# Column-tiled broadcasts of the second modulation, a new dense order, and a moved last norm in a fused attention and token-mixing kernel

## The chip, the cores and the metric

The kernel runs on one core of one Trainium2 chip. The metric is the device time of one execution in microseconds, lower is better. Before the change three runs took 251.43, 252.77 and 253.32 us; the median is 252.77. One profiled execution took 251.73 us, of which the profile's span (first to last instruction) is 250.0; times inside the profile are counted from the start of the span.

## The reference

One transformer-like block over x of 2048 rows by 512 columns (bf16), with six modulation vectors from a conditioning vector c:

```python
mod = (silu(c) @ w_mod).reshape(1, 6, 1, 512)
sa, ca, ga, sb, cb, gb = mod[:, 0], ..., mod[:, 5]
h = layernorm(x) * (1 + ca) + sa
x = x + ga * A(h)        # A: 32 heads of 16, causal, window of 256 rows, softmax, then @ wo
h = layernorm(x) * (1 + cb) + sb
x = x + gb * B(h)        # B: layernorm again, then u = gelu(w1.T @ h + b1), y = w2.T @ u + b2
```

B mixes rows: w1 is 2048 x 1792 and w2 1792 x 2048, and the 512 columns pass through side by side. So every row block of h (16 blocks of 128 rows) must be there before u is complete, but the sum over the row blocks can be begun with those that are.

## The kernel before

**Stages.** Rows go in 16 blocks of 128 (`tb`), four blocks make a row group (`tg`, 0 to 3). The preamble (to about 13 us) makes the first modulation and the first query and key block. Then comes the attention part (to about 160 us): 76 units, (group, block of 8 heads, piece of the window), in a fixed order. Each unit is: scores on TensorE (`emit_scores`, lines 616 and 628, the latter for the mask), two exponentials of 128x1024 on ScalarE (`emit_exp`, line 639), and after the units of eight heads the values (`emit_av`, line 656), which VectorE transposes and divides by the row sums (`norm_out` line 667, `norm_rest` lines 680 to 691). After 160 us comes the tail: the last four output projections (`t_wo`, lines 1115 and 1119), the last norms (`t1`, `t2`, `t3`), the first product of B (lines 1094 and 1187), GELU (1104), and the second product (line 1211) with the output (1218 to 1224).

**Dense groups.** Between the scores, TensorE is given dense groups, each four matmuls of 128x512 into one of two PSUM banks, and an evacuation: `k`, `q` and `v` blocks (`qk_group`, `v_group`; k12 is group 1, block of heads 2; v7 is row block 7), output projections `wo` of a row block (`wo_group`, line 412; the residual is added at 418), the transposed biases (`bias`), and the broadcasts `bc` (`bc_group`, lines 385 to 397). `ORDER` (line 739) lists them; `run_dense` takes the first of the list that is ready. When none is ready it makes a part sum (`part_group`, line 453): matmuls of w1 by the row blocks of h that are there, for 10 of the 14 column blocks of w1 (`PART`) and row blocks below 10 (`NB`), at least four at a time. What was summed in this way is left out of the sums in the tail. After a `wo` group a chain of small norm steps (`ln23`, lines 696 to 727) makes the row block of h: the norm of the residual, times 1 + cb, plus sb, and the second norm. Its statistics are on VectorE, three small steps on GpSimd (POOL; lines 217, 220, 224), the rest on either.

**The broadcasts.** ga, cb, sb and gb are needed as rows that are the same in all 128 partitions. A group makes each: the conditioning vector, replicated to 128 columns (`sT_rep`, line 583), is the stationary operand, and a 512-wide part of w_mod moves, so all 128 output rows are equal. VectorE copies the result (adding 1 for cb). ga is then folded into the projection weights (`fold_wod`, line 947, four operations), cb and sb are used in `ln23`, gb at line 1218. A `wo` group needs the folded weights, cb and sb.

**The planner.** The order of instructions is written at build time by a planner (`Plan`) with a clock for each engine (`pl.pe`, `pl.dve`, `pl.pool`, `pl.sp`) and prices for each step; `ready` holds when a result is expected. `fill` runs chain steps on VectorE until a given time, `drain` the evacuations, `force` makes what the next unit needs. All loads and copies by DMA are issued by SP in program order; an instruction on SP that waits holds up those behind it. The keys of head blocks 2 and 3 of groups 1 to 3 are copied into the `KT` ring by eight DMAs (line 369), the value blocks are swapped between partition halves by two (line 313), the normed rows are transposed by DMA (line 301), and w1 is loaded where other weights have been used up (lines 965 to 983). `PLAN` (line 756) holds six of its settings.

**The end of the attention.** After the last values, the planner ran all leftover chain steps (`while pl.chains: fill(...)`), and then came the tail.

## Time and profile before

| | before |
|---|---|
| three runs, us | 251.43, 252.77, 253.32 |
| profiled execution, us | 251.73 |
| its span, us | 250.0 |
| granted TensorE clock | 0.998 |
| first exponential begins, last ends, us | 13.05, 159.24 |
| exponentials on ScalarE, busy us (line 639) | 139.7 in 152 |
| second product of B on TensorE, chain share (line 1211) | 19% |
| part sums ahead, from ... to, us (line 453) | 121.5 to 158.8 |

Engines are written PE (TensorE), PEld (its weight loads), DVE (VectorE), ACT (ScalarE), POOL (GpSimd), SPq (SyncE, issuing DMAs). In a timeline a row has the start in us, the length in us, engine, line and operation, what it writes and reads, shapes, the number of instructions that were merged, and in brackets how long the engine had been idle and what ended that. A matmul record of 128x512 lasts about 0.38 us, but such matmuls overlap and follow each other every 0.22 us; some records are missing, and weight loads are counted in full.

### The profile page before, as it was taken

What the parts mean: (1) busy time and instruction counts of PE and PEld (TensorE: products, weight loads), DVE (VectorE), ACT (ScalarE), POOL (GpSimd) and SP (SyncE); (2) the same over time, 40 slices, a digit from 0 to 9 for tenths busy, and PEclk for the clock granted to TensorE, in tenths of its full rate; (3) what the DMA queues carried; (4) which work ended last, traced back from release to release, by engine and by line L of the source; (5) the groups of instructions that cost most, each with busy time, mean ns of one, the idle gap of its engine ahead of it and who ended that gap; (6) DMA issues with size and microseconds to landing.
All of it is one profiled execution on the core that took longest, in us unless ns stands there. A gap on an engine that the chain in (4) does not pass through costs nothing.

```text
span 250.0 us, 8264 instructions
## 1 busy us (share of the span) xinstructions
PE 229.4 (92%) x3547; PEld 119.2 (48%) x3585; DVE 181.1 (72%) x363; ACT 160.2 (64%) x183; POOL 108.3 (43%) x222
## 2 busy tenths in 40 slices
PE   6888897999899999899999999979999999999994
PEld 2543554445445545545545545534444444444443
DVE  5988999988799799989899999869624404150643
ACT  2285999998899999999999999703564400000000
POOL 7325462216748629866878789337600000000000
PEclk9999999999999999999999999999999999999999
DMA  5986994064630255000359300699950000111121
GB/s 177 318 265 161 142 326 153 9 127 83 193 139 5 51 91 88 5 3 3 60 84 335 94 0 5 207 393 414 409 200 0 0 0 21 65 41 43 45 84 43
DMA packets 31977, 30.49 MB, mean 122 GB/s; under 512 B 15940, under 2 KB 26564, under 8 KB 31940
## 3 DMA queue, kind: packets, MB, share of 16 engines
q1 hardware_dynamic: 31940, 29.96, 41.2%
q8 instruction: 28, 0.46, 0.7%
q14 instruction: 9, 0.07, 0.1%
HBM read 22.03 MB, written 2.10 MB: 96 GB/s over the span
## 4 chain that ended last, share of the span: by engine, by line
PE 52%; ACT 23%; DVE 11%; SPq 5%; DMA 4%; issue 2%; POOL 2%; POOLq 0%; DVEq 0%; ACTq 0%
ACT et L639 23%; PE py L1211 19%; PE pu L1094 6%; PE pss L616 5%; PE pu L1187 5%; PE dn L453 4%; PE dn L322 4%; PE dn L345 4%; DMA x<-in_A_x_dram 2%; SPq L369 2%; DVE KT L375 2%; DVE t L667 2%; PE pss L628 2%; DVE ln_stats L236 1%; SPq L123 1%
## 5 line engine op out<-in xcount | busy, mean ns | idle before, releaser
L639 ACT ACTIVATE et<-pss 128x1024 bf16<-128x1024 f32 (+1 forms) x152 | 139.7, 1037 | 6.7 <-PE pss L628 6.2
L1211 PE MATMUL py<-guT,w2r 128*128 128x512 bf16 (+1 forms) x234 | 48.3, 366 | 0.2
L616 PE MATMUL pss<-QT,KT 32*128 32x64 bf16 (+3 forms) x720 | 37.2, 254 | 4.7 <-ACT et L639 1.8
L1211 PEld LDWEIGHTS <-w2r 128*128 128x128 bf16 x238 | 23.3, 98 | 25.3
L1218 DVE SCALAR_TENSOR_TENSOR o<-py,bFM,bc_gb 128x512 bf16<-128x512 f32 (+1 forms) x17 | 11.7, 716 | 30.5 <-PE py L1211 30.5
L345 PE MATMUL dn<-h1T,wqkv 128*128 128x512 bf16 x111 | 31.1, 381 | 1.8 <-issue 1.1
L616 PEld LDWEIGHTS <-KT 32*128 32x128 bf16 x720 | 14.2, 92 | 34.3 <-issue 22.7
L217 POOL TENSOR_SCALAR ln_ve<-ln_mv 128x1 f32<-128x1 f32 (+1 forms) x40 | 9.3, 232 | 43.0 <-DVE ln_mv L237 19.9
L667 DVE STREAM_TRANSPOSE t<-pss 128x512 f32<-128x512 f32 x32 | 20.9, 691 | 4.3 <-PE pss L656 4.3
L656 PE MATMUL pss<-et,VaugT 64*32 64x320 bf16 (+4 forms) x720 | 20.8, 253 | 1.1 <-ACT et L639 0.6
L656 PE MATMUL pss<-et,Vx 64*32 64x320 bf16 (+4 forms) x720 | 20.9, 254 | 0.0
L628 PE MATMUL pss<-mask_rown,mask_hown 32*128 32x128 bf16 (+1 forms) x304 | 20.6, 206 | 0.0
L656 PEld LDWEIGHTS <-VaugT 64*32 64x32 bf16 x720 | 18.7, 91 | 3.8 <-issue 3.3
L683 POOL TENSOR_TENSOR merge<-t,zr 128x512 bf16<-128x512 f32 x13 | 13.8, 1059 | 15.4 <-DVE zr L680 15.3
L628 PE MATMUL pss<-mask_rfar,mask_hfar 32*128 32x64 bf16 (+1 forms) x304 | 19.8, 200 | 0.0
L220 POOL TENSOR_TENSOR ln_rb<-ln_ve,mhalf 128x1 f32<-128x1 f32 x32 | 18.3, 572 | 2.7
L656 PEld LDWEIGHTS <-Vx 64*32 64x32 bf16 x720 | 17.8, 91 | 1.4 <-issue 0.6
L322 PE MATMUL dn<-wqkv,h1T 128*128 128x512 bf16 x58 | 16.0, 380 | 2.0 <-DVE sT_rep L583 0.7
L1102 DVE TENSOR_TENSOR gelu_a<-pu,part 128x512 f32<-128x512 f32 x10 | 6.4, 686 | 13.4 <-PE pu L1187 8.2
L453 PE MATMUL dn<-hb,w1hi 128*128 128x512 bf16 x51 | 14.5, 381 | 0.5 <-issue 0.3
L345 PEld LDWEIGHTS <-wqkv 128*128 128x128 bf16 x120 | 9.6, 97 | 10.7 <-DVE KT L375 0.7
L691 DVE STREAM_TRANSPOSE OTd<-merge 128x512 bf16<-128x512 bf16 x16 | 11.2, 699 | 1.2 <-POOL merge L683 1.2
(130 smaller groups left out, 366.9 us busy)
## 6 DMA issues: line engine op xcount, KB each, us to landing
w2r<-in_B_w_dram SPq DMA_DIRECT2D x14, 512.0 KB, 10.2
wmod<-in_w_mod_dram SPq DMA_DIRECT2D x12, 256.0 KB, 4.7
w1b<-in_B_w_dram SPq DMA_DIRECT2D x6, 448.0 KB, 7.3
Vx<-VaugT SPq DMA_DIRECT2D x16, 147.5 KB, 2.5
x<-in_A_x_dram SPq DMA_DIRECT2D x16, 128.0 KB, 3.6
w1hi<-in_B_w_dram SPq DMA_DIRECT2D x6, 320.0 KB, 4.8
out_dram<-otile SPq DMA_DIRECT2D x15, 128.0 KB, 1.7
wqkv<-in_B_w_dram SPq DMA_DIRECT2D x4, 320.0 KB, 3.9
```

What stands on the lines that cost most here:

```text
L220: nc.gpsimd.tensor_tensor(out=r, in0=ve[:], in1=mhalf[:, 0:n], op=ALU.pow)
L322: nc.tensor.matmul(pv[:], lhsT=h1T[tg][:, dc, tl * P : (tl + 1) * P], rhs=wqkv[:, dc, 2 * D : 3 * D], start=(dc == 0), stop=(dc == ND - 1),)
L345: nc.tensor.matmul(pq[:], lhsT=wqkv[:, dc, col0 : col0 + P], rhs=h1T[tg][:, dc, :], start=(dc == 0), stop=(dc == ND - 1),)
L453: nc.tensor.matmul(ps[:], lhsT=w1_of(s0 + n, fc), rhs=hb[s0 + n][:], start=(n == 0), stop=(s0 + n + 1 == s1),)
L616: nc.tensor.matmul(pss[j // 2][:, j % 2, 64 * at : 64 * (at + c1 - c0)], lhsT=Kring[kh // 8 % 3][rows, g8, kh % 8].rearrange("p n t -> p ( ...
L628: nc.tensor.matmul(o[:, at[0] : at[-1] + 1 : step, :], lhsT=mask_h[name][rows].rearrange("p n t -> p (n t)"), rhs=mask_r[name][rows, :].un ...
L639: nc.scalar.activation(out=state["e", tg, g8, ui][:, 2 * a : 2 * a + 2, 0:n], in_=state.pop((u, a))[:, :, 0:n], func=ACT.Exp, scale=SCORE_ ...
L656: nc.tensor.matmul(state["po"][32 * j : 32 * j + 32, par, 64 * c0 : 64 * c1], lhsT=v[:, h * DV : h * DV + 32], rhs=state["e", tg, g8, ui][ ...
L667: nc.vector.transpose(out=state["t2"][:, par, :], in_=state["po"][:, par, :])
L683: eng.tensor_tensor(out=m[:].rearrange("p (b a d) -> p a b d", a=2, d=DH), in0=t2v[:, :, :, 0:DH], in1=zr[:].to_broadcast([P, 2, 16, DH]), ...
L1094: nc.tensor.matmul(pu[fc][:], lhsT=w1_of(sc, fc), rhs=hb[sc][:], start=(sc == done.get(fc, 0)), stop=(sc == NT - 1),)
L1211: nc.tensor.matmul(pys[n][:, c0:c1], lhsT=w2r[:, fc, tb * P : (tb + 1) * P], rhs=guT[fc][:, c0:c1], start=(fc == gelus[0]), stop=(fc == ge ...
```

## The change

1. **Broadcasts.** One group replaces four. Each of its four steps runs four matmuls, one for each of ga, cb, sb and gb, into 32 output columns each at column positions 0, 32, 64 and 96 of the array; `sT_rep` has 32 columns. VectorE copies the bank once, adding 1 in the rows of cb by a per-partition scalar. SP then writes four rows to DRAM and reads them back, replicated to all partitions, into one tile `bc_all`. All four quarters of w_mod and both loads of wo must be there before the group starts.
2. **The order.** A new `ORDER`, new `PLAN` settings, and changed prices of the planner's clocks.
3. **q01 on ScalarE.** The groups named in `PLAN[6]` (here q of group 0, head block 1) are evacuated by an activation with Copy on ScalarE.
4. **The end of the attention.** Of each leftover chain all but its last step run before the tail; the last step (the second norm of a row block, `n3`) runs after the second residual of the tail. Loads that are still listed are issued at the end of the attention.

```diff
-    bc_cb1 = const.tile([P, D], DT.bfloat16, name="bc_cb1")
-    bc_sb = const.tile([P, D], DT.bfloat16, name="bc_sb")
-    bc_gb = const.tile([P, D], DT.bfloat16, name="bc_gb")
+    bc_all = const.tile([P, 4, D], DT.bfloat16, name="bc_all")
+    bc_ga, bc_cb1, bc_sb, bc_gb = (bc_all[:, n, :] for n in range(4))
+    outside = ctx.enter_context(tc.tile_pool(name="outside", bufs=1, space=bass.MemoryType.DRAM))
+    bc_rows = outside.tile([4, D], DT.bfloat16, name="bc_rows")
...
-    sT_rep = modw.tile([P, ND, P], DT.bfloat16, name="sT_rep")
+    sT_rep = modw.tile([P, ND, 32], DT.bfloat16, name="sT_rep")
+    bc_row = modw.tile([P, D], DT.bfloat16, name="bc_row")
+    add_row = modw.tile([P, 1], DT.float32, name="add_row")
+    nc.gpsimd.memset(add_row[:], 0.0)
+    nc.gpsimd.memset(add_row[32:64, :], 1.0)
...
+    def copy_of(key):
+        return functools.partial(nc.scalar.activation, func=ACT.Copy) if key in PLAN[6] else nc.vector.tensor_copy
...
-                nc.vector.tensor_copy(out=QT[tg][g8][:], in_=pq[:])
+                copy_of((kind, tg, g8))(out=QT[tg][g8][:], in_=pq[:])
...
-    def bc_group(v, dst, add1, then=()):
+    BC = (2, 4, 3, 5)
+    def bc_group(then):
         def mm(ps_b, k):
-            nc.tensor.matmul(
-                ps_b[:], lhsT=sT_rep[:, k, :], rhs=wmod_of(v)[:, k, :],
-                start=(k == 0), stop=(k == ND - 1),
-            )
+            for n, v in enumerate(BC):
+                nc.tensor.matmul(
+                    ps_b[32 * n : 32 * n + 32, :], lhsT=sT_rep[:, k, :], rhs=wmod_of(v)[:, k, :],
+                    start=(k == 0), stop=(k == ND - 1), tile_position=(0, 32 * n), skip_group_check=True,
+                )
         def evac(ps_b):
-            if add1:
-                nc.vector.tensor_scalar_add(out=dst[:], in0=ps_b[:], scalar1=1.0)
-            else:
-                nc.vector.tensor_copy(out=dst[:], in_=ps_b[:])
-        return Group(ND, mm, evac, 0.65, [("w", v)] + [("w", "o")] * (v == 2), ("bc", v), then=then)
+            nc.vector.tensor_scalar_add(out=bc_row[:], in0=ps_b[:], scalar1=add_row[:])
+            dma.dma_start(out=bc_rows[:], in_=bc_row[0:P:32, :])
+            dma.dma_start(out=bc_all[:], in_=bc_rows[:].unsqueeze(0).to_broadcast([P, 4, D]))
+        return Group(ND, mm, evac, 0.65, [("w", v) for v in BC] + [("w", "o")], ("bc",), us=0.27, then=then)
...
-            v1 k20 wo3 q31 v2 q10 q22 k21 q33 wo11 wo6 v0 q02 wo0 q21 k11 q30 k10 bc2 v3 k01 v7
-            v6 v15 wo8 q01 q20 bias k33 q32 v10 k13 wo7 wo9 q03 v4 v8 q11 v5 k02 wo5 k12 v9 k31
-            v14 q23 bc3 v13 wo2 k30 bc0 q13 v12 wo10 k22 v11 bc1 wo1 q12 wo4 k32 k23 k03
+            k10 v13 v12 q32 wo4 wo5 bias k20 wo8 q23 q30 wo11 v1 v0 q20 v9 v3 v2 k22 k01 q10 q01
+            k33 k30 v7 k02 v11 q02 v6 v14 v5 k11 v15 q11 wo10 k23 k03 v10 wo9 k13 v4 v8 wo6 wo1
+            q31 q22 q21 k31 q03 k12 q13 k21 bc wo2 wo7 wo3 q12 k32 q33 wo0
...
-        PLAN = (0.2, 8.0, 5.0, 0.4, 0.6, 0.2)
+        PLAN = (2.0, 16.0, 8.0, 0.4, 0.3, 0.2, (('q', 0, 1),))
...
-        ready["w", "b"], pl.sp = 8.0, 5.0
+        ready["w", "b"], pl.sp, pl.dve = 8.0, 5.6, 2.5
...
+                    if g.gives == ("bc",):
+                        issue(pl.dve, 0.65)
+                        pl.sp += 2.0
+                        landed = issue(pl.dve, 0.65) + 0.5
+                        for v in BC:
+                            ready["bc", v] = landed
+                        add_chain(g.then, ready["bc", 2])
+                        return
...
-            pl.pe += 1.1 if tg == 0 else 1.38
+            pl.pe += 1.05 if tg == 0 else 1.33
...
-                st = lambda g: [(lambda tl=tl: ln1_stats(g, tl), 0.82, 0.1, None) + (1.5,) * (tl % 2) for tl in range(4)]
+                st = lambda g: [(lambda tl=tl: ln1_stats(g, tl), 0.85, 0.1, None) + (1.5,) * (tl % 2) for tl in range(4)]
...
-                pl.pe += 0.37
-                scored = pl.pe + 0.25
+                pl.pe += 0.33 if late else 0.4
+                scored = pl.pe + 0.22
...
         emit_av(NG - 1, ND - 1, (4,), False, True)
+        while loads:
+            o, i, key = loads.pop(0)
+            dma.dma_start(out=o, in_=i)
         norm_out(0)
...
-        while pl.chains:
-            fill(pl.dve + 9.0)
+        while any(len(chain[0]) > 1 for chain in pl.chains):
+            for chain in pl.chains:
+                if len(chain[0]) > 1:
+                    run(chain)
...
         for step in range(5):
             if step < 4:
                 t_wo(12 + step)
+            if step == 1:
+                for chain in pl.chains:
+                    run(chain)
             if step:
                 t1(11 + step)
```

Not shown: the prices of the dense evacuations (0.65 to 0.66, masked keys 1.35 to 1.33, the fold 0.33 to 0.40), the clock of ScalarE's copy in the planner, and the places that read the broadcasts, which now read parts of `bc_all`.

## The prediction

> **What bounds the kernel now.** I read the page's busy table first, then ScalarE's timeline, then a table of stretches, then the two groups of matmuls that matter, the chain of waits, and last the timelines around 23 and 166 us.
>
> ```profile
> span 250.0 us, 8264 instructions
> ...
> PE 229.4 (92%) x3547; PEld 119.2 (48%) x3585; DVE 181.1 (72%) x363; ACT 160.2 (64%) x183; POOL 108.3 (43%) x222
> ```
>
> TensorE is busy 92% of the span, 20.6 us idle. In the attention part (13 to 160 us) ScalarE looks like the bound: its exponentials, by its timeline:
>
> ```profile
> 23.93 21.03 ACT L639 ACTIVATE et<-pss 128x1024 bf16<-128x1024 f32 x24 [2.97 <-PE pss L628]
> 45.18 14.86 ACT L639 ACTIVATE et<-pss 128x1024 bf16<-128x1024 f32 x16 [0.21 <-PE pss L628]
> 61.08 3.77 ACT L639 ACTIVATE et<-pss 128x1024 bf16<-128x1024 f32 x4 [1.04 <-PE pss L628]
> 65.86 93.38 ACT L639 ACTIVATE et<-pss 128x1024 bf16<-128x1024 f32 x100 [1.01 <-PE pss L628]
> ```
>
> The brackets are the idle time before each piece: with 0.45 and 0.24 at the start, 5.9 us in all. But a gap of ScalarE isn't by itself a gap of the kernel. While ScalarE waits, TensorE works on dense groups, and what it does not get done before 160 us it does after. The stretches show how full it is in the end of the attention:
>
> ```profile
> 125.00:140.00 15.00, 14.68 (x289) 7.64 (x295) 13.94 (x28) 14.96 (x17) 11.63 (x21) 1.00 0.73 203
> 140.00:150.00 10.00, 9.71 (x229) 5.33 (x224) 9.10 (x18) 9.96 (x12) 8.18 (x15) 1.00 0.06 16
> 150.00:160.00 10.00, 9.74 (x263) 5.61 (x264) 9.60 (x20) 9.19 (x10) 7.86 (x14) 1.00 0.19 56
> ```
>
> (Columns: length, busy PE, PE weight loads, DVE, ACT, POOL, granted clock, DMA.) TensorE is at 97 to 98%, VectorE at 91 to 96%, at full clock. The filler there is line 453, part sums of the MLP's first product, made ahead:
>
> ```profile
> L453 PEld LDWEIGHTS <-w1hi x56: 95/98/99, 121.5 to 157.9; 128*128 128x128 bf16 x56
> ...
> L453 PEld LDWEIGHTS <-wqkv x19: 95/98/99, 145.9 to 158.6; 128*128 128x128 bf16 x19
> ```
>
> 75 weight loads, so 75 such matmuls, of the 100 that the code allows (10 column blocks times 10 row blocks): 25 more could be made ahead. After 160 us the chain is TensorE's own to the end. So the time is TensorE's work plus its idle time, and a slot saved in the attention shortens the tail by one slot. The price of a slot is in the chain, 10.74 / 49 = 0.219 us, with the price of packed small matmuls ahead of it:
>
> ```profile
> 159.16 1.36 PE pss L656 x95
> ...
> 173.39 10.74 PE pu L1094 x49
> ```
>
> **Part 1, the broadcasts on TensorE.** Removed: four groups of four matmuls of 128x512 (line 387: 16 weight loads, 14 records), 16 x 0.219 = 3.50 us. Added: four steps of four matmuls, each 32 output columns wide, side by side. The trace has no four-column tiles over 128 rows; the nearest row is line 656, eight tiles of 64 rows by 32 columns. One such group has 12 pieces with 2560 columns in all for each of eight tiles; one after another they would take 8 x 2560 x 0.219 / 512 = 8.76 us, and the chain shows 1.36: 6.4 of 8, or 80%. So a step costs 0.219 / 0.8 = 0.274, four cost 1.10, saved 2.40. Bounds: full overlap saves 3.50 - 0.88 = 2.6; no overlap saves nothing, and if each of 16 loads (98 ns, this line's row) then stands free too, it loses 1.6. I take 2.4, because line 656 has the same column tiles.
>
> In the Trainium skill, "TensorE: Matmul & The Clock Gate", Part 3, says that weight loads overlap running matmuls only where their row groups differ. By that rule these four tiles, which share all rows, would gain less, down to nothing. The trace speaks against it: at 159.25 to 159.40 loads of line 656 for column tiles of the same row half run while matmuls that began at 159.24 last until 159.54. The rule as a rival is below.
>
> The 2.40 us become 2.40 / 0.219 = 11 more part sums ahead; the room is 25. Cover: VectorE must empty them (0.69 us for each group of 4 or more). It gains its own time: evacuations 0.692 + 0.692 + 0.679 + 0.675 = 2.74 become one of 0.68; the copy that replicates the conditioning vector (0.42) shrinks to a quarter of its elements (nearest 128x128 rows 0.34, so 0.1 saved); the copy of q01 (0.68) leaves. That is 2.8 us, four evacuations' worth, so the 11 sums are covered, and I book nothing more for VectorE. Without this cover the 2.4 is 0.
>
> **Part 2, the broadcasts by DMA.** SP issues one write to DRAM and one replicating read. Issues on SP cost 0.4 to 0.6 each; a write to DRAM lands in 1.5 to 1.7 us (the output's rows); the second waits on SP for the first, and 0.5 MB to 128 partitions takes 3.7 (0.25 MB of wod) to 7.3 (0.45 MB of w1b), I take 5. So SP stands 0.6 + 1.7 + 0.6 = 2.9 us, and the fold of wod begins about 8 us after the evacuation. Before, all four broadcasts were out at 59.6 and the first of line 412's projections ran at 62.5. All four quarters of wmod were issued by 35.9, so the group can run from about 41. If it does, SP's queue is empty (nothing issued from 37.2 to 48.6) and the wait costs nothing. If it runs between 48 and 64, four transposes, four swaps and the eight copies into KT (56.71 to 63.82) stand behind it. Nothing, then, to 2.9; I take 0. The fold itself keeps its four operations (median 0.42).
>
> **Part 3, the norm behind the residuals.** VectorE and TensorE at the seam:
>
> ```profile
> 164.75 0.18 DVE L706 BATCH_NORM_AGGREGATE ln_mv<-ln_stats 128x2 f32<-128x6 f32 x1
> 166.28 0.41 DVE L228 TENSOR_SCALAR hb<-hb,ln_rb 128x512 bf16<-128x512 bf16 x1 [1.35 <-POOL ln_rb L224]
> 166.61 1.28 DVE L1119 TENSOR_TENSOR x<-pa,x 128x512 bf16<-128x512 f32 x2
> ```
>
> ```profile
> 163.91 1.89 PE L1115 MATMUL pa<-wod,OTd 128*128 128x512 bf16 x8
> 167.35 1.89 PE L1115 MATMUL pa<-wod,OTd 128*128 128x512 bf16 x8 [1.55 <-DVE x L1119]
> ```
>
> VectorE waits 1.35 for POOL's three small steps, and then the first residual waits for the last norm. With the norm behind the second residual, the first can begin at 164.93 and end by 165.6; TensorE's first two projections end at 165.80. Its 1.55 us go. The norm's 0.41 stays, behind two residuals, where POOL has long finished (166.25). Next late would be the norms of the last four blocks, but 19 + 49 matmuls of line 1094 stand ahead of them. Bounds: 0 (the new order leaves another leftover) to 1.7. I take 1.55.
>
> **Part 4, the new order and q01 on ScalarE.** The longest gap of ScalarE ends in TensorE's timeline so:
>
> ```profile
> 22.91 0.17 PE L401 MATMUL dn<-identity,b 30*128 30x30 bf16 x1 [0.73 <-DVE KT L375]
> 23.41 0.40 PE L616 MATMUL pss<-QT,KT 32*128 32x320 bf16 x8 [0.34 <-DVE QT L353]
> ```
>
> Before, q02 (copy at 19.57), v3, both masks of k01 and q01 pass VectorE in a row. The new order has v0 to v3, k01, q01 with no q02 between, and q01's copy runs on ScalarE, idle there, beside the masks. VectorE sheds 0.66 + 0.68, TensorE 0.88. The scores come some 1.3 us earlier, and of the 1.07 us of TensorE's idle time I take 0.9 as gone. The copy on ScalarE costs about 0.6 (half an exponential of 1.05, a 512-wide one being 0.69 at line 1104): nothing while ScalarE is waiting, at most 0.6 later. For the other 50 places of the order I have no row: TensorE's named waits from 14 to 122 us sum to 8.9, and the longest stretches are 38 to 44 (1.37 idle) and 62 to 68 (0.99). The planner's new constants go both ways against the rows: fold 0.33 to 0.40 (row 0.42) and statistics 0.82 to 0.85 (0.86) nearer; masked evacuation 1.35 to 1.33 (1.41 in the chain) and values 1.38 to 1.33 (1.36) no nearer. I take 0, bounds -3 to +3.
>
> **Sum.** -2.4 - 1.55 - 0.9 = -4.85. The profiled execution took 251.73 (span 250.0 and 1.73 around it): 246.9. It lies 1.04 under the median of the three runs (252.77), from which the sum gives 247.9. I say 247.5, between.
>
> **Rivals.** (a) *The saved slots don't arrive*: the column tiles don't overlap, or VectorE, over 91% busy, has no room to empty more part sums. For it: that share, and the missing exact row. Against: line 656, and 2.8 us off VectorE. Only 2.45 is left: 249.3 to 250.3; with all 16 loads standing free too, 251 to 252. By the rule quoted above from the Trainium skill the time would be in this case.
> (b) *The order does more*: up to 3 us of TensorE's idle time before 122 us go: 244.5. For it: 8.9 us of named waits. Against: nothing shows which.
> (c) *Slower: copies into KT come late.* For groups 1 to 3 the keys of two heads' blocks go by eight DMAs on SP. From evacuation to scores: 0.69 + 5.3 to 7.1 (issues) + 2.3 (landing), about 9 us. Before, group 1's were already late: ScalarE lost 1.04 and 1.01. The new order puts k12 and k32 near its end, and SP has 2.9 us of broadcast wait on top. It decides from the point where the evacuation comes less than 9 us ahead of its unit. TensorE then runs only what dense work is ready, and before 121 us there are no part sums. One such wait in full: 247.5 + 9 = 256.5; half covered by dense work, 252. Against: in groups 2 and 3 the copies were issued from 93.7 and 122.7 and cost no gap.
>
> **Numbers.** Forecast 0.48, (a) 0.22, (b) 0.13, (c) 0.17. A difference under 1% (2.5 us) can't be told from none here, as the three runs spread over 1.9. Faster by over 1% (under 250.2): forecast, (b), and a bit of (a): 0.64. Within 1%: the rest of (a), a covered (c): 0.21. Slower: 0.15. Range: 244 (b) to 254 (part of (c)); the forecast's own range is 245.5 to 249.5.
>
> **What would show it.** The broadcast group in some 1.1 us of TensorE with four matmuls starting together; about 86 weight loads at line 453 in place of 75, and so many fewer at 1094 and 1187; no wait for the residual at line 1115; ScalarE's gap near 23 us at half its length, with one 128x512 copy in it; SP's second broadcast issue some 2 us behind the first. I am wrong if line 453 stays at 75 while TensorE's idle time grows, if ScalarE's gaps sum to more than 5.9 us, or if a copy into KT ends a wait of over 2 us.

## The result and the profile after

The changed kernel took 258.9, 258.92, 259.18 and 262.9 us, median 259.05, beside a median of 252.5 for the kernel before on the same chip: ratio 1.0262, 95% interval [1.0234, 1.029]. A second measurement, on another chip, gave 261.75 (260.35 to 263.3) against 252.12: 1.0355 [1.0297, 1.0414]. The forecast was 247.5 us, a gain. It is slower by 6.5 to 9.6 us.

The ratios leave disturbed executions out, the medians don't; the profiled one, of 262.9 us at a mean granted clock of 0.972 (0.987 to 0.997 in the other three), is such a one, and some 4 us of its span of 261.2 are its own. At a clock of 0.997 the kernel still took 258.9 us, so most of the loss is not the clock's. A profile on the second chip (span 261.6, clock 0.974) shows the waits at the value swap (3.39) and at the residual (2.86) again, on which the readings below rest, but not the one of 1.74 at 142.2.

The busy table and the row of the granted clock, of the changed kernel:

```profile
span 261.2 us, 8314 instructions
...
PE 238.9 (91%) x3585; PEld 121.6 (47%) x3585; DVE 177.6 (68%) x364; ACT 160.6 (62%) x184; POOL 101.6 (39%) x215
...
PEclk9999979999999988799999799999999999999999
```

TensorE's busy time went up, by 9.5 us, though it has less to do: the slices with a 7 and an 8 in the clock's row are stretches in which the same matmuls take longer (1 - 0.972 of 261.2 is 7.3 us). A part of the 9.5 is only that the profile before lacks 38 matmul records (3547 and 3585, with 3585 weight loads in both). ScalarE's timeline of the changed kernel, its longer pieces from 20 us on:

```profile
21.65 0.60 ACT L363 ACTIVATE QT<-dn 128x512 bf16<-128x512 f32 x1 [1.38 <-PE dn L355]
...
98.68 9.27 ACT L652 ACTIVATE et<-pss 128x1024 bf16<-128x1024 f32 x10 [3.58 <-PE pss L641]
109.04 31.58 ACT L652 ACTIVATE et<-pss 128x1024 bf16<-128x1024 f32 x34 [1.09 <-PE pss L641]
...
144.65 1.94 ACT L652 ACTIVATE et<-pss 128x1024 bf16<-128x1024 f32 x2 [1.92 <-PE pss L641]
147.82 18.80 ACT L652 ACTIVATE et<-pss 128x1024 bf16<-128x1024 f32 x20 [1.23 <-PE pss L641]
```

The gap near 23 us did shrink (1.38 and a copy of 0.60, against 2.97). New gaps of 3.58, 1.92, 1.23 and 1.09 took its place; the last exponential ends at 147.82 + 18.80 = 166.62 instead of 159.24. What ended the largest is in SP's timeline of the changed kernel (the issues between 50 and 98 us):

```profile
55.97 6.97 SPq L379 DMA_DIRECT2D KT<-k  x8
63.05 0.59 SPq L408 DMA_DIRECT2D bc_rows<-bc_row  x1
64.74 0.37 SPq L409 DMA_DIRECT2D bc_all<-bc_rows  x1
...
77.75 5.67 SPq L379 DMA_DIRECT2D KT<-k  x8
83.47 0.60 SPq L1012 DMA_DIRECT2D w1hi<-in_B_w_dram  x1
84.17 1.16 SPq L319 DMA_DIRECT2D Vx<-VaugT  x2
85.37 3.30 SPq L1012 DMA_DIRECT2D w1hi<-in_B_w_dram  x4
88.76 1.10 SPq L319 DMA_DIRECT2D Vx<-VaugT  x2
89.97 8.07 SPq L307 DMA_TRANSPOSE h1T<-xn  x4
```

Before, SP's timeline has these issues in another order:

```profile
63.93 2.91 SPq L983 DMA_DIRECT2D w1hi<-in_B_w_dram  x6
...
86.33 6.02 SPq L301 DMA_TRANSPOSE h1T<-xn  x4
...
93.71 5.28 SPq L369 DMA_DIRECT2D KT<-k  x8
```

The wait that follows, in TensorE's timeline of the changed kernel:

```profile
95.54 0.16 PE L297 MATMUL dn<-identity,Vx 128*128 128x1 bf16 x1 [2.44 <-DMA Vx<-VaugT]
```

Five loads of w1 (`w1hi`), 320 KB each, are issued from 83.5 to 88.7, between the value swaps (`Vx`) and right ahead of the four transposes of group 3. Before, they were out by 66.8, and the transposes began at 86.33, ahead of group 2's KT copies (93.71). Now the transposes take 8.07 us to issue instead of 6.02, a swap issued at 88.76 keeps TensorE waiting until 95.5, and the clock drops behind that wait, as stretches of 2 us of the changed kernel show (length, busy PE, granted clock, DMA share, GB/s):

```profile
93.00:95.00 2.00, 0.10 (x11) 1.00 1.46 97
95.00:97.00 2.00, 1.46 (x50) 0.80 0.65 131
97.00:99.00 2.00, 2.00 (x82) 0.50 0.38 74
99.00:101.00 2.00, 2.00 (x27) 0.85 0.00 0
```

At the other end, the part sums and the first residual of the tail (the group of weight loads by form; TensorE's timeline):

```profile
L466 PEld LDWEIGHTS <-w1hi 128*128 128x128 bf16 x59 | 5.2, 101 | 6.0 <-issue 1.4
L466 PEld LDWEIGHTS <-wqkv 128*128 128x128 bf16 x9 | 0.9, 98 | 1.0
```

```profile
176.26 1.89 PE L1151 MATMUL pa<-wod,OTd 128*128 128x512 bf16 x8 [2.86 <-DVE x L1155]
```

59 + 9 = 68 part sums, not 75 and far from the 86 forecast; they begin at 129.9 instead of 121.5. The wait for the first residual, which was to go, grew from 1.55 to 2.86.

**A ledger.** Three numbers of a profile account for most of the span in the kernels below: when the last exponential ends, how many part sums were made by then (each missing one costs 0.219 us in the tail), and TensorE's wait for the first residual. Their sum against the kernel before, and the span against the 250.0 of before:

| kernel | median us, ratio | last exponential ends | part sums | residual wait | sum of the three | span - 250.0 |
|---|---|---|---|---|---|---|
| changed (second profile) | 261.75, 1.0355 | 166.34 | 68 | 2.9 | +10.0 | +11.6 |
| hold_w1 | 257.36, 1.0199 | 162.44 | 68 | 2.9 | +6.1 | +7.0 |
| after_pool | 262.68, 1.0377 | 166.83 | 68 | 2.9 | +10.5 | +11.3 |
| order_alone | 261.4, 1.034 | 164.61 | 65 | 4.5 | +10.5 | +12.1 |
| seam_alone | 250.57, 0.9929 | 159.06 | 75 | 0 | -1.7 | -1.8 |
| bc_alone | 265.22, 1.0501 | 174.71 | 87 | 0 | +11.3 | +11.8 |
| bc_alone_pool | 258.71, 1.0255 | 168.97 | 87 | 0 | +5.6 | +5.6 |
| bc_first | 258.62, 1.0147 | 161.77 | 64 | 0.3 | +3.7 | +3.8 |
| bc_first_pool | 253.61, 1.0034 | 162.66 | 64 | 0.3 | +4.6 | +4.7 |

(Changed kernel: 166.34 - 159.24 = 7.10; 7 x 0.219 = 1.53; 2.9 - 1.55 = 1.35; together 9.98.) The medians come from several runs and the other columns from one execution, so where the runs spread they need not agree: the profile of bc_first is of its fastest run (255.5 of 255.5 to 262.08), that of bc_first_pool of its slowest (256.38 of 251.44 to 256.38). The ledger fails for hold_w1_deep (162.34, 68 and 0): it gives +3.1, the span is 9.9 longer, and 5.0 of the rest are the two waits of the first product shown below.

### The profile page after: what moved, and what is told of

Its sections match the earlier page's. It is cut to its first block, busy times and chain, and to the rows that moved or that the text cites. A ratio compares the mean times of both kernels' runs of the same rounds, so it can differ in the third digit from the quotient of the medians.

```text
span 261.2 us, 8314 instructions
## 1 busy us (share of the span) xinstructions
PE 238.9 (91%) x3585; PEld 121.6 (47%) x3585; DVE 177.6 (68%) x364; ACT 160.6 (62%) x184; POOL 101.6 (39%) x215
## 4 chain that ended last, share of the span: by engine, by line
PE 49%; ACT 23%; DVE 8%; DMA 6%; SPq 5%; POOL 3%; issue 3%; POOLq 0%; DVEq 0%; ACTq 0%
ACT et L652 23%; PE py L1251 19%; PE pu L1227 6%; PE pss L629 5%; PE pss L669 5%; PE dn L466 4%; PE dn L355 4%; PE dn L332 3%; DMA wqkv<-in_A_wqkv_dram 3%; DMA Vx<-VaugT 2%; PE dn L425 2%; SPq L379 2%; PE pss L641 2%; DVE t L680 2%; POOL ln_rb L226 1%
## 5 line engine op out<-in xcount | busy, mean ns | idle before, releaser
L652 ACT ACTIVATE et<-pss 128x1024 bf16<-128x1024 f32 (+1 forms) x152 | 139.7, 1045 | 12.4 <-PE pss L641 12.1
L629 PE MATMUL pss<-QT,KT 32*128 32x64 bf16 (+3 forms) x720 | 40.1, 259 | 7.2 <-ACT et L652 3.9
L355 PE MATMUL dn<-h1T,wqkv 128*128 128x512 bf16 x120 | 34.0, 393 | 0.0
L629 PEld LDWEIGHTS <-KT 32*128 32x128 bf16 x720 | 15.7, 92 | 37.9 <-issue 27.6
L1258 DVE SCALAR_TENSOR_TENSOR o<-py,bFM,bc_all 128x512 bf16<-128x512 f32 (+1 forms) x17 | 11.7, 715 | 30.5 <-PE py L1251 30.5
L669 PE MATMUL pss<-et,VaugT 64*32 64x320 bf16 (+4 forms) x720 | 22.2, 267 | 1.1 <-ACT et L652 0.4
L669 PE MATMUL pss<-et,Vx 64*32 64x320 bf16 (+4 forms) x720 | 22.2, 267 | 0.0
L641 PE MATMUL pss<-mask_rown,mask_hown 32*128 32x128 bf16 (+1 forms) x304 | 21.8, 211 | 0.0
L332 PE MATMUL dn<-wqkv,h1T 128*128 128x512 bf16 x64 | 17.3, 389 | 1.2 <-DMA wqkv<-in_A_wqkv_dram 1.2
L466 PE MATMUL dn<-hb,w1hi 128*128 128x512 bf16 x59 | 17.3, 406 | 0.0
L732 POOL TENSOR_TENSOR hb<-hb,bc_all 128x512 bf16<-128x512 bf16 x12 | 14.2, 1192 | 0.8 <-DVE hb L732 0.4
```

Source lines behind the costliest of these rows:

```text
L332: nc.tensor.matmul(pv[:], lhsT=h1T[tg][:, dc, tl * P : (tl + 1) * P], rhs=wqkv[:, dc, 2 * D : 3 * D], start=(dc == 0), stop=(dc == ND - 1),)
L355: nc.tensor.matmul(pq[:], lhsT=wqkv[:, dc, col0 : col0 + P], rhs=h1T[tg][:, dc, :], start=(dc == 0), stop=(dc == ND - 1),)
L466: nc.tensor.matmul(ps[:], lhsT=w1_of(s0 + n, fc), rhs=hb[s0 + n][:], start=(n == 0), stop=(s0 + n + 1 == s1),)
L629: nc.tensor.matmul(pss[j // 2][:, j % 2, 64 * at : 64 * (at + c1 - c0)], lhsT=Kring[kh // 8 % 3][rows, g8, kh % 8].rearrange("p n t -> p ( ...
L641: nc.tensor.matmul(o[:, at[0] : at[-1] + 1 : step, :], lhsT=mask_h[name][rows].rearrange("p n t -> p (n t)"), rhs=mask_r[name][rows, :].un ...
L652: nc.scalar.activation(out=state["e", tg, g8, ui][:, 2 * a : 2 * a + 2, 0:n], in_=state.pop((u, a))[:, :, 0:n], func=ACT.Exp, scale=SCORE_ ...
```

## The experiments

In all of them the lines with a plus are those of the kernel that ran, and `...` stands for lines left out. Ratios are against the kernel before on the same chip, with 95% intervals.

**The changed kernel again**, unaltered, as the yardstick of the first batch (after_again).

> The changed kernel unaltered, for a profile of an undisturbed execution. The first profile had waits of TensorE at 93 us (2.4, swapped values), 103 to 106 us (about 3, no dense work), 142 us (1.7) and at the residual (2.9), and a clock of 0.50 for some 3 us behind several of them. If the clock is the cause, a profile at full clock has few of these waits. If the waits are the cause and the clock only follows them, they are there again at a mean clock of 0.99 or more, and the span is near 257.

261.75, 1.0355 [1.0297, 1.0414]. Its profile has a clock of 0.974, so the profile at full clock that the expectation asks for is missing, and it decides neither reading.

**The w1 loads held back** (hold_w1). TensorE's program is that of the changed kernel; only the six loads move behind the transposes of group 3.

```diff
-            if "pool" not in w1 and not loads and all(k in ready for k in modulation):
+            if "pool" not in w1 and not loads and all(k in ready for k in modulation) and ("x", 3, 3) in ready:
```

> Only the place of six loads of w1 in the program changes: they are listed after the last transposed block of group 3 instead of before. Theory L (late loads collide): in the changed kernel the late broadcast puts five of these loads, 1.6 MB, at 83.5 to 88.7 us beside a swap of values (6.1 us to land in place of 2.5) and four transposes (8.1 us in place of 6.0). Without them there the wait of 2.4 us at 93 and ScalarE's gap of 3.6 shrink below 1, group 3 starts 3 us earlier, and the time falls by 3 to 5 us, to 254 to 256. Rival O (the order packs badly by itself): the waits move elsewhere, and the time stays within 1.5 of 259.

257.36, 1.0199 [1.0146, 1.0251]. SP's and ScalarE's timelines of this kernel:

```profile
89.95 6.40 SPq L307 DMA_TRANSPOSE h1T<-xn  x4
96.40 4.17 SPq L1012 DMA_DIRECT2D w1hi<-in_B_w_dram  x6
```

```profile
66.04 39.32 ACT L652 ACTIVATE et<-pss 128x1024 bf16<-128x1024 f32 x42 [0.90 <-PE pss L641]
```

The transposes take 6.40 instead of 8.07, 42 exponentials run through where the 3.58 stood, and 4.4 of the 9.6 us come back (3.9 by the ratios). The fall of 3 to 5 us came, the 254 to 256 did not. The same hold with the broadcasts on POOL's queue (hold_w1_pool against after_pool, below) gives 4.2, or 3.1 by the ratios. So the collision of the loads with the swap and the transposes is shown as a cause, of 3 to 4 us. Whether it acts by the 3.9 us of issues ahead of the swap or by the traffic, the edit does not separate. The part sums stay at 68 and the residual wait at 2.9: those have another cause.

**The moved norm alone** (seam_alone), on the kernel before.

```diff
-        while pl.chains:
-            fill(pl.dve + 9.0)
+        while any(len(chain[0]) > 1 for chain in pl.chains):
+            for chain in pl.chains:
+                if len(chain[0]) > 1:
+                    run(chain)
...
+            if step == 1:
+                for chain in pl.chains:
+                    run(chain)
```

> The kernel before with the moved last norm alone (one leftover chain). By the prediction's step: TensorE's wait of 1.55 us for the first residual goes, the first residual ends before 165.8, and the time is 1.0 to 1.6 lower, 251.0 to 251.6 against 252.5. Rival: the wait goes but the next norms on VectorE and POOL, whose work is the same, end last; then less than 0.5 is gained.

250.57, 0.9929 [0.9904, 0.9955]: 0.7% faster than the kernel before. TensorE's and VectorE's timelines of this kernel:

```profile
163.73 3.70 PE L1117 MATMUL pa<-wod,OTd 128*128 128x512 bf16 x16
```

```profile
164.79 0.69 DVE L1121 TENSOR_TENSOR x<-pa,x 128x512 bf16<-128x512 f32 x1
165.66 0.69 DVE L1121 TENSOR_TENSOR x<-pa,x 128x512 bf16<-128x512 f32 x1 [0.17 <-PE pa L1117]
166.26 0.40 DVE L228 TENSOR_SCALAR hb<-hb,ln_rb 128x512 bf16<-128x512 bf16 x1
```

All 16 projections now run without a wait, and the norm stands at 166.26 behind two residuals that end by 166.35.

**Is the whole chain of leftovers better behind the residuals?** The same two lines, with every leftover step at step 1 instead of only the last: on seam_alone (seam_deep, 3 steps) and on hold_w1 (hold_w1_deep, 15 steps).

```diff
-        while any(len(chain[0]) > 1 for chain in pl.chains):
-            for chain in pl.chains:
-                if len(chain[0]) > 1:
-                    run(chain)
...
-                for chain in pl.chains:
-                    run(chain)
+                while any(chain[0] for chain in pl.chains):
+                    for chain in pl.chains:
+                        run(chain)
```

> The kernel seam_alone with all three leftover steps behind the second residual. There the first residual can begin at the end of the last transposition, 164.1, in place of 164.9, but TensorE's first two projections end only at 165.8, so nothing more should be won: within 0.3 us of seam_alone. If the norms of the last blocks were the bound it would be slower.

> The kernel hold_w1 with all 15 leftover norm steps of the three row blocks behind the second residual of the tail, in place of 12 ahead of the first residual and 3 behind. If the leftovers ahead of the residual are what the tail loses: TensorE's wait of 2.9 us for the first residual falls below 0.5, and the time by 1.5 to 2.9 us against hold_w1. Rival: VectorE's work is only moved; the norms of the last four row blocks end as late, and less than 0.7 is gained.

251.83, 0.999 [0.9963, 1.0017], and 260.95, 1.0348 [1.0314, 1.0382]: 1.3 and 3.6 us worse than without. The residual wait is gone in both, but the norms of the last four row blocks stand behind the leftovers, and the first product now comes later by those. In seam_deep the last 36 matmuls ahead of line 1191 take 9.04 us, from 174.78 to 183.82, where seam_alone has 7.77. The waits of TensorE in hold_w1_deep (total, times, longest):

```profile
PE pu L1127 <- ACT hb L1166: 3.6, 1, 3.6
...
PE pu L1127 <- DVE hb L234: 1.4, 1, 1.4
```

So with several leftover row blocks the price is VectorE's and POOL's chain of norms, ahead of the residual or behind it; moving it, in these two kernels, did not remove it.

**The copy of q01 on ScalarE** (seam_q01), on seam_alone: the group's evacuation by an activation with Copy.

```diff
-                nc.vector.tensor_copy(out=QT[tg][g8][:], in_=pq[:])
+                (functools.partial(nc.scalar.activation, func=ACT.Copy) if (kind, tg, g8) == ("q", 0, 1) else nc.vector.tensor_copy)(out=QT[tg][g8][:], in_=pq[:])
```

> The kernel seam_alone with the copy of q01 on ScalarE and everything else in place, the order too. ScalarE waits there for 2.98 us, until both masks of k01 and then q01 have passed VectorE. With q01 beside the masks the scores come 0.6 us earlier; ScalarE pays 0.6 inside its own wait. Expected: the gap up to the next exponential, the copy counted in it, 0.4 to 0.7 shorter, and 0 to 0.6 us of time.

250.52, 0.9935 [0.9911, 0.9959], that is, seam_alone's time. ScalarE's gap went from 2.98 to 2.06 and a copy of 0.60, that is 0.3 shorter with the copy counted, where 0.4 to 0.7 was expected; no time came of it.

**The new order without the new broadcasts** (order_alone): the changed kernel with the four old groups where `bc` stood.

```diff
-            q31 q22 q21 k31 q03 k12 q13 k21 bc wo2 wo7 wo3 q12 k32 q33 wo0
+            q31 q22 q21 k31 q03 k12 q13 k21 bc0 bc1 bc2 bc3 wo2 wo7 wo3 q12 k32 q33 wo0
```

> The changed kernel with the four old broadcast groups in place of the one (listed at its place in the new order) and so without the two DMAs; the new order, clocks, q01 on ScalarE and the moved norm stay. If the late broadcast by DMA is the main cause: the loads of w1 go out by 70 us, the wait for the swapped values at 93 is gone, and the time is 250 to 254. If the new order is the cause by itself: 256 to 260 again, with as many leftover steps at 160 us.

261.4, 1.034 [1.0283, 1.0397]: as slow as the whole change, with no broadcast DMA in it. SP's, ScalarE's and TensorE's timelines of this kernel:

```profile
80.37 5.30 SPq L374 DMA_DIRECT2D KT<-k  x8
85.76 2.78 SPq L314 DMA_DIRECT2D Vx<-VaugT  x4
89.91 6.53 SPq L302 DMA_TRANSPOSE h1T<-xn  x4
```

```profile
67.16 39.11 ACT L644 ACTIVATE et<-pss 128x1024 bf16<-128x1024 f32 x42 [0.94 <-PE pss L633]
```

```profile
175.41 3.57 PE L1139 MATMUL pa<-wod,OTd 128*128 128x512 bf16 x8 [4.45 <-DVE x L1143]
```

Group 2's KT copies and all swaps go ahead of group 3's transposes here, too, but ScalarE runs 42 exponentials unbroken across them, and the w1 loads are out at 68.1. So neither that order of the queue nor the collision is what costs here. The first projection comes at 82.3 instead of 62.5, though the fold is done at 52.9 and cb and sb are out at 60.3; there are 65 part sums, and four leftover row blocks, whose steps stand ahead of the first residual. The planner laid out another program than in the changed kernel, so this shows what the new order and settings can cost with the broadcasts at this late place, not their exact share in the change.

**The new broadcasts without the new order** (bc_alone: on the kernel before, the group listed where the first of the four stood; bc_alone_pool: the two DMAs on POOL's queue; bc_seam_pool: that, with the moved norm).

```diff
-            v1 k20 wo3 q31 v2 q10 q22 k21 q33 wo11 wo6 v0 q02 wo0 q21 k11 q30 k10 bc2 v3 k01 v7
+            v1 k20 wo3 q31 v2 q10 q22 k21 q33 wo11 wo6 v0 q02 wo0 q21 k11 q30 k10 bc v3 k01 v7
...
-            dma.dma_start(out=bc_rows[:], in_=bc_row[0:P:32, :])
-            dma.dma_start(out=bc_all[:], in_=bc_rows[:].unsqueeze(0).to_broadcast([P, 4, D]))
+            nc.gpsimd.dma_start(out=bc_rows[:], in_=bc_row[0:P:32, :])
+            nc.gpsimd.dma_start(out=bc_all[:], in_=bc_rows[:].unsqueeze(0).to_broadcast([P, 4, D]))
```

> The kernel before with the new broadcast group alone, in the first of the four places of the old order, all clocks of the planner as before. By the prediction's steps 1 and 2: TensorE is 2.6 us shorter in the broadcasts, about 11 more part sums are made ahead (86 weight loads in place of 75), and the time falls by 2 to 2.6. Theory L's part: the group must wait for all four quarters of the weights and then for two DMAs, so the first fold begins 8 to 12 us later than 40.8, the first projection 5 to 10 us later than 62.5, and dense work runs out in between; then the time does not fall and may rise by 1 to 4.

> The kernel before with the new broadcasts alone (old order, old settings, listed at the first of the four old places), the pair issued by POOL. With SP it took 265.2: the pair stood between two transposes of group 1 and ahead of its value swap, and ScalarE waited 6.8 us. Theory (what stands behind the pair on SP is its whole price, and the column tiles' 2.4 us reach the end): the gap falls under 2.5 us, 250 to 253. Rival (one late group instead of four early ones is a price by itself: fold, cb and sb come later, fewer part sums, later residuals): the gap falls but the time stays over 255.

> As bc_alone_pool, with the moved last norm. Theory (column tiles gain): below the moved norm alone, 248 to 250. Rival (the saved slots don't arrive): no better than the moved norm alone (250.6), or worse by what bc_alone_pool is over the kernel before.

In this order: 265.22, 1.0501 [1.045, 1.0553]; 258.71, 1.0255 [1.0214, 1.0297]; 260.0, 1.0307 [1.0267, 1.0346]. ScalarE's timeline of bc_alone:

```profile
67.89 3.77 ACT L647 ACTIVATE et<-pss 128x1024 bf16<-128x1024 f32 x4 [6.77 <-PE pss L636]
...
137.46 37.25 ACT L647 ACTIVATE et<-pss 128x1024 bf16<-128x1024 f32 x40 [6.48 <-PE pss L636]
```

and of bc_alone_pool, with SP's issues behind it:

```profile
63.28 35.54 ACT L647 ACTIVATE et<-pss 128x1024 bf16<-128x1024 f32 x38 [2.61 <-PE pss L636]
...
131.72 37.25 ACT L647 ACTIVATE et<-pss 128x1024 bf16<-128x1024 f32 x40 [6.48 <-PE pss L636]
```

```profile
95.89 5.96 SPq L374 DMA_DIRECT2D KT<-k  x8
101.95 2.56 SPq L306 DMA_TRANSPOSE h1T<-xn  x2
```

Off SP's queue, the first gap fell from 6.77 to 2.61 and 6.2 us came back (0.0246 of the ratio): in bc_alone the pair stood between the third and the fourth transpose of group 2 and ahead of a value swap. The 13 us that bc_alone lost are more than either reading allowed (4 at most). The second gap stayed at 6.48 to the digit, so it isn't the pair's place on SP. What the trace shows is that the last two transposes of group 3 are issued behind the KT copies of group 2, group 3's `h1T` is ready at 114.4 (100.1 before), and its projections run in one burst while ScalarE waits; no run moved that chain. The theory's 250 to 253 fell, and the rival (one late group by itself) named another reason than the one found. There are 60 + 27 = 87 part sums, and no residual wait. That these are the saved slots isn't shown: in bc_alone_pool the part sums begin at 110.0 instead of 121.5, with the projections of group 3 still to come, and the attention ends 9.7 us later than before. The moved norm adds nothing there, since it has nothing left to remove.

**Where the pair stands** (bc_first: the changed kernel with `bc` at the front of the order; bc_first_pool: with the pair on POOL's queue; after_pool and hold_w1_pool: the changed kernel and hold_w1 with the pair on POOL's queue). The edit for POOL is the one above.

```diff
-            k10 v13 v12 q32 wo4 wo5 bias k20 wo8 q23 q30 wo11 v1 v0 q20 v9 v3 v2 k22 k01 q10 q01
+            bc k10 v13 v12 q32 wo4 wo5 bias k20 wo8 q23 q30 wo11 v1 v0 q20 v9 v3 v2 k22 k01 q10 q01
...
-            q31 q22 q21 k31 q03 k12 q13 k21 bc wo2 wo7 wo3 q12 k32 q33 wo0
+            q31 q22 q21 k31 q03 k12 q13 k21 wo2 wo7 wo3 q12 k32 q33 wo0
```

> The changed kernel with the broadcast group moved from the end of the order to its front, nothing else. Theory L: the group runs some 8 us earlier (48 in place of 56), the fold is done by 60 in place of 74, the loads of w1 go out before 70 and not beside the swap at 84, and the time falls by 3 to 5 us against the changed kernel, if the pair of DMAs does not now stand ahead of the transposes and the copies into KT; if it does, ScalarE has a gap of 3 us or more between 50 and 70 and half of the gain is lost.

> The kernel bc_first with its two broadcast DMAs issued by POOL in place of SP; the same bytes. In bc_first the pair stands on SP between the third and the fourth transpose: 1.7 us from the write's issue to the next, the transpose at 53.9 in place of 51.6, the swap of values at 56.2, which lands at 60.6, and ScalarE has a gap of 5.6 us. If the wait in SP's queue is the price: the swap is issued 2 to 3 us earlier, the gap shrinks below 3, and the time falls by 2 to 3 us against bc_first. If the price is the 0.5 MB on the DMA engines beside the transposes and the swap, the swap still lands late and the gap stays above 4.

> The changed kernel with one edit: the pair of broadcast DMAs is issued by POOL. Every other engine's program is the same. In the changed kernel the pair was issued on SP at 63.05 and 64.74, 5.3 us after its evacuation, behind eight KT copies; the next SP work behind it, at 77.75, was not held up. Theory (the pair's price in this kernel is only its late begin; the collision of the w1hi loads with the swap and the transposes is what costs, and stays): the fold begins 4 to 6 us earlier, part sums 68 to 72, ScalarE's gap before 98.7 stays over 2 us; time 0.5 to 2 us less than the changed kernel. Rival (the wait in SP's queue is the price here too, as in the kernel with the pair first): 4 to 6 us less, and the gap goes.

> As the kernel with the held w1hi loads, with the pair issued by POOL. Theory: the same 0.5 to 2 us as without the hold, so 255.5 to 257. Rival (queue wait and collision are the same price told twice): no gain at all over the held loads, 257.4.

In this order: 258.62, 1.0147 [1.007, 1.0225]; 253.61, 1.0034 [1.0003, 1.0064]; 262.68, 1.0377 [1.033, 1.0424]; 258.49, 1.0256 [1.0203, 1.031]. The chain of waits in bc_first (start, length, what) shows how the pair holds up the queue:

```profile
51.62 1.68 DMA bc_rows<-bc_row
...
53.36 0.37 SPq L409
...
53.85 2.19 SPq L307
...
57.14 3.42 DMA Vx<-VaugT
```

SP stands 1.7 us until the rows have landed, the fourth transpose waits behind it, then the swap, then ScalarE for 5.62 us. On POOL's queue the four transposes are issued unbroken (48.70 to 54.71) and the gap shrinks to 2.40; the move gains 2.9 us by the ratios, give or take 2 (5.0 by the medians). The same bytes are moved, so the queue is the price here. Listing the group first was by itself worth 5.2 us by the ratios, in spite of the gap of 5.62. Both edits together give back 8.1 of the 9.0 us that the changed kernel lost (0.0321 and 0.0355 of 252), through another layout of the planner: the fold begins at 58.8, the first projection at 63.6, and one row block is left over. In the changed kernel the pair stands at 63.05 to 65.1, with one load behind it and then nothing until 77.75, and there the move gains nothing (262.68 against 261.75, 258.49 against 257.36, in different batches). POOL issued it there at 57.27 and 59.53, but VectorE folded from 69.6, no earlier than from 68.8 with SP: the rows' earlier arrival moved nothing, as the fold keeps its place in VectorE's program. So of my expectation for after_pool neither the 0.5 to 2 us nor the earlier fold came; that the pair's wait on SP is not the price here held.

**What the pair costs as such** (dummy_ga, dummy_gb): the kernel before, unaltered in what it computes, with the same pair of DMAs added behind the evacuation of ga or of gb, into a tile that nothing reads (the diff is of dummy_ga; in dummy_gb `v == 5`).

```diff
+            if v == 2:
+                dma.dma_start(out=bc_rows[:], in_=dst[0:P:32, :])
+                dma.dma_start(out=bc_all[:], in_=bc_rows[:].unsqueeze(0).to_broadcast([P, 4, D]))
```

> The kernel before, plus the two DMAs of the broadcast (a 4 KB write to DRAM and the 0.5 MB replicating read) into a tile that nobody reads, issued behind the evacuation of ga at about 35 us. Everything else is as before. There SP has the last loads of weights in its queue until 37 us and nothing from 37 to 48. Theory: the DMAs cost by what stands behind them on SP and beside them on the DMA engines, so here they cost 0 to 1 us. Rival: the pair costs the same wherever it stands.

> The same two extra DMAs, issued behind the evacuation of gb at 56.6 us, ahead of the eight copies into KT. Theory: the copies start 2 to 3 us later than 56.7 (issue, wait for the write, issue) and land beside 0.5 MB more, the scores of group 1 that read them come later by that, ScalarE's gap at 65 us grows from 1.0 to 3 to 5 us, and the time rises by 2 to 4 us. Rival: the dense work covers it, under 1 us.

255.17, 1.0104 [1.0074, 1.0133], and 252.45, 0.9988 [0.996, 1.0017]. I had the two the wrong way round. Behind ga the pair stood ahead of loads that were needed soon. Behind gb it stood behind the copies into KT (56.70 to 64.30), not ahead of them, and delayed only the w1 loads, from 63.9 to 70.0, which no part sum needed before 122. SP's timeline and a wait of TensorE, of dummy_ga:

```profile
35.52 0.60 SPq L401 DMA_DIRECT2D bc_rows<-bc_ga  x1
37.21 0.35 SPq L402 DMA_DIRECT2D bc_all<-bc_rows  x1
37.62 2.48 SPq L989 DMA_DIRECT2D wmod<-in_w_mod_dram  x5
```

```profile
PE dn L390 <- DMA wmod<-in_w_mod_dram: 2.2, 1, 2.2
```

Five loads of w_mod stand behind the pair, and TensorE waits 2.2 us for one of them. Before, all six were issued from 31.23 to 35.9. SP waits twice here: 4.2 us for the evacuation of ga, which ends at 35.5, and 1.0 us for the rows, so most of this price is an issue that stood in the queue before its data were there.

## Why the prediction was wrong, step by step

The saving on TensorE was sized rightly. The steps that failed are the two terms that I took at 0: the broadcasts by DMA (part 2) and the new order (part 4).

**Part 1, column tiles: right on TensorE, and a little cautious.** The steps of the group, in TensorE's timeline and in its group, of the changed kernel:

```profile
56.17 0.83 PE L401 MATMUL dn<-wmod,sT_rep 128*32 128x512 bf16 x12
57.39 0.40 PE L401 MATMUL dn<-wmod,sT_rep 128*32 128x512 bf16 x4
```

```profile
L401 PEld LDWEIGHTS <-sT_rep x16: 92/94/97, 56.2 to 57.4; 128*32 128x32 bf16 x16
```

Three steps of four matmuls begin and end within 0.83 us, the last of them lasting some 0.39: (0.83 - 0.39) / 2 = 0.22 us a step, 0.88 for four, so the bound of full overlap, 2.6 us saved, and not the 2.4 taken. The rule of the Trainium skill ("TensorE: Matmul & The Clock Gate", Part 3) that weight loads overlap only with other row groups does not hold here: these tiles share all rows, and no load stands free, with 16 loads of 92 to 97 ns in those 0.88 us. That these slots become "11 more part sums" isn't shown: bc_alone and bc_alone_pool made 87, 12 more than 75, but in a longer attention part. In the changed kernel the 11 did not arrive.

**Part 2, the broadcasts by DMA: "I take 0" failed.** The bounds "nothing, then, to 2.9" counted the time in which SP stands, not what stands behind it. By its place it cost nothing (dummy_gb), 2.5 us (dummy_ga, 255.17 - 252.72), 2.9 (bc_first) and 6.2 (bc_alone), the last two with a transpose and a swap behind it, and in dummy_ga mostly by the wait for the evacuation. In the changed kernel itself the queue's wait is worth nothing, by after_pool; what costs is that the one group is listed late: w_mod was issued by 35.9, and bc_first made the group at 47. Its evacuation came at 57.8, the fold at 68.8 instead of 40.7, line 425's first projection at 79.6 instead of 62.5, and the w1 loads, which need those buffers, at 83.5, in the way of a swap and of the transposes. I read that "all four broadcasts were out at 59.6" and did not follow the fold and its loads from there. That collision is 3 to 4 us by the two holds.

**Part 3, the moved norm: right alone, undone by part 4.** Forecast -1.55, measured -1.55 by the medians (252.12 - 250.57) and -1.8 by the ratio and in the profile. In the change it met the bound that I had named ("0, the new order leaves another leftover") and went past it: three row blocks were left, 12 steps stood ahead of the first residual, and the wait became 2.86, so a loss of 1.3 where the bound was 0. The next late are the norms of the last four blocks, as named, and there is little slack ahead of them: two more steps behind the residuals cost 1.3 us (seam_deep), twelve more 3.6 (hold_w1_deep).

**Part 4, the order: "I take 0, bounds -3 to +3" failed.** order_alone lost 8.7 us (261.4 against 252.72 on its chip) without any new broadcast DMA, with the four old groups at the late place. What I had not priced is that with a late group the projections come late and row blocks are left over: four in order_alone and three in the changed kernel, with first projections at 82.3 and 79.6, but one in bc_first and bc_first_pool, with 65.2 and 63.6. (Each is another layout of the planner, so this is read from four kernels and not isolated.) The copies of group 2 into KT go ahead of group 3's transposes in all of these, so they are not the price: bc_first_pool has them so (81.12 and 90.71) and stands at 1.0034. The part sums stay low there too (64, beside 65 and 68), so those go with the order and its settings; 11 of them are 2.4 us. The 0.9 us for the gap near 23 us came as a shorter gap, but seam_q01 shows that such a gap is worth no time when TensorE stays as busy.

**The rivals.** Case (c), an operation late on SP with 252 to 256.5, was nearest. It named the right queue and the wrong victims: the value swap and the transposes of group 3 were late, while the longest wait for a copy into KT was 0.5 us. That its price of 9 lies near the measured loss is luck, since the collision on the queue is 3 to 4. Two of my signs of error were met: part sums below 75 while idle time grew, and ScalarE's gaps above 5.9 us (11.8).

**Open.** With the loads held, hold_w1 is still 5.2 us above the kernel before. In its profile, of its slowest execution (+7.0), 1.5 are part sums, 1.35 the residual wait, and the attention ends 3.2 later; of this last I have no single cause. bc_first_pool, with the group early, lacks most of this loss, but what its layout changed isn't taken apart. TensorE also stood 1.74 us at 142.2 in the changed kernel for nothing that the profile shows, and did not on the second chip. And order, settings and broadcasts can't be separated exactly, since the planner turns every edit into another program.

The best version found is the kernel before with the moved norm alone, at 0.9929 [0.9904, 0.9955].

## What to carry to other kernels

A DMA that waits on its queue, for its data or for another DMA, costs what stands behind it there, here from nothing to 6 us for the same pair: list what is queued behind it before taking it at 0, and put such a pair on a queue whose next work is far off. A group that is merged from several becomes ready with the last of its inputs and makes everything behind it late; follow its first consumer, the buffers which that frees and the loads into them, before counting the slots it saves. Where a planner lays out the program, test each part alone, for a gain of 1.6 us was here hidden under a layout that cost 9.

## What was not expected of the hardware

A wait of 2.44 us on TensorE was followed by a granted clock of 0.80, 0.50 and 0.85 in three stretches of 2 us, in an execution where the stretch ahead of it had 1.00: 0.4 + 1.0 + 0.3 = 1.7 us more of loss behind the wait itself. In dummy_ga a wait of 2.15 us was followed by 0.60 and 0.54. The Trainium skill ("TensorE: Matmul & The Clock Gate", the table under "Why this matters for your kernels") asks for no idle gaps above about 3 us; in these two traces shorter ones were followed by the drop. The length of one wait doesn't decide it alone: behind the wait of 2.86 us for the residual the clock stayed at 1.00 (176 to 180 us) in the first profile of the changed kernel and fell to 0.67 and 0.50 there in the second. What decides it, no run here shows.

A value swap beside five loads of 320 KB took 6.1 us to land (median of all swaps 2.5), and four transposes took 8.07 us to issue instead of 6.02.
